# Attention with a cached K and V: keys-by-queries scores in 32-row tiles, probabilities as weights of P.V, sums from a ones column beside V

## The chip, the cores and the metric

The kernel runs on one core of a Trainium2 chip. The metric is device microseconds (us) of one execution. Before the change the kernel takes 501.62 us (median of 3 runs, 500.74 to 503.49). TensorE, which is named PE in the profile, does something nearly all the time (96% of the span).

## The reference, cut to what matters

```python
B, Sq, D = 8, 112, 640            # batches, queries, model width
H, Sk, Dh = 32, 512, 192          # heads, keys, head width; everything in bfloat16

def reference(x, k_cache, v_cache, wq, wo):
    q = (x @ wq).reshape(B, Sq, H, Dh).transpose(0, 2, 1, 3)
    scores = einsum("bhqd,bhkd->bhqk", q, k_cache) * Dh ** -0.5
    p = softmax(scores)
    o = einsum("bhqk,bhkd->bhqd", p, v_cache)
    return o.transpose(0, 2, 1, 3).reshape(B, Sq, H * Dh) @ wo
```

There are 256 pairs of a batch and a head. K and V are 8 x 32 x 512 x 192 x 2 bytes = 50.3 MB each, read once. In what follows a *unit* is four heads of one batch, so there are 64 units.

## The kernel before

Work goes in pairs of heads. K is brought in by DMAs that transpose on the way, so that the head width, over which the scores contract, lies on the partitions (the rows of SBUF, the on-chip memory). Scores have queries on partitions. So the softmax runs along the free axis, and the probabilities then have to be transposed for P.V. That is done by a matmul with a diagonal matrix of reciprocal sums, which also normalises.

```python
# scores of one head: queries x keys, two halves of 256 keys, contraction 192 in two chunks
pe.matmul(bk[:, 0:256], qs[:, qb, EA[h], :], ktb[:, :, 0, cs], start=True, stop=False)
pe.matmul(bk[:, 0:256], qs[:, qb, ET[h], :], ktb[:, :, 1, cs], start=False, stop=True)
pe.matmul(bk[:, 256:512], qs[:, qb, OC[h], :], ktb[:, :, 2, cs], start=True, stop=False)
pe.matmul(bk[:, 256:512], qs[:, qb, OH[h], :], ktb[:, :, 1, cs], start=False, stop=True).then_inc(sS, 1)
...
# transposing and normalising the probabilities with diagonals
for j in range(4):
    mm = pe.matmul(ps[:, 2 + h, j * SQ:(j + 1) * SQ], p_sb[:, pslot, j * 128:(j + 1) * 128],
                   dg[:, dslot, :], start=True, stop=True)
...
# row maximum on VectorE (it also copies the scores to SBUF)
dve.tensor_scalar(s_sb[:, Hh % NSS, :], ps[0:SQ, h, :], -scale, None, op0=ALU.mult,
                  op1=ALU.min, accum_out=nmx[:, Hh % NS:Hh % NS + 1]).then_inc(dSM, 1)
...
# K of four heads (sync engine)
src = k_cache[b, h0:h0 + G].rearrange("u (r q) d -> (u r) (q d)", q=4)
dst = kt[kb][:].rearrange("p a m c -> p (a m) c")
sp.dma_start_transpose(dst, src).then_inc(mK[kb], 16)
```

Of the kernel before, what the change touches and what calls it, by code (L numbers as in the profile page):

```python
# [5 lines left out]

BF16 = mybir.dt.bfloat16
F32 = mybir.dt.float32
ACTF = mybir.ActivationFunctionType
ALU = mybir.AluOpType  # L10

DEFAULT_ORDERS = dict(
    PE=[("S", 0), ("PT0", -1), ("PV", -2), ("PT1", -1), ("O", -3), ("Q", 2)],
# [7 lines left out]
def build_mha_kernel(nc, x, k_cache, v_cache, wq, wo, out, cfg=None):  # L21
    cfg = dict(cfg or {})
    B, SQ, D = x.shape
    _, H, SK, DH = k_cache.shape
# [3 lines left out]
    DC = D // 128  # L28
# [8 lines left out]
    scale = float(DH) ** -0.5  # L37
# [31 lines left out]

    with ExitStack() as es:  # L70
        def sb(name, shape, dt):
            return es.enter_context(nc.sbuf_tensor(name, shape, dt))

        def sem(name):
            return es.enter_context(nc.semaphore(name))

        WQC = HG * DH
        wq_sb = sb("wq_sb", [128, 2, DC, WQC], BF16)
        wo_sb = sb("wo_sb", [128, 2, 3 * PPU, D], BF16)
        OUTT = cfg.get("OUTT", False)  # L80
        if OUTT:
            accT = sb("accT", [128, B, DC, SQ], F32)
            oTf = sb("oTf", [128, 2, DC, SQ], BF16)
            acc = None
        else:
            acc = sb("acc", [SQ, B, D], F32)
        xT_sb = sb("xT_sb", [128, DC, B * SQ], BF16)
        kt = [sb(f"kt{j}", [128, 2, 3, G * 128], BF16) for j in range(NKB)]
        vt = [sb(f"vt{j}", [128, G, 768], BF16) for j in range(NVB)]
        qs = sb("qs", [128, NQ, NSLOT, SQ], BF16)  # L90
        s_sb = sb("s_sb", [SQ, NSS, SK], F32)
        p_sb = sb("p_sb", [SQ, NP, SK], BF16)
# [4 lines left out]
        ident = sb("ident", [128, 128], BF16)  # L97
        nmx = sb("nmx", [SQ, NS], F32)
        rsum = sb("rsum", [SQ, NS], F32)
        rinv = sb("rinv", [SQ, NS], F32)  # L100
        ps = es.enter_context(nc.psum_tensor("ps", [128, 8, 512], F32))

        sS = sem("sS"); sPT = sem("sPT"); sPV = sem("sPV"); sO = sem("sO"); sQ = sem("sQ")
        dSM = sem("dSM"); dDG = sem("dDG"); dQC = sem("dQC"); dPTE = sem("dPTE"); dOA = sem("dOA"); dRC = sem("dRC")
        aEX = sem("aEX"); aQE = sem("aQE"); aPTE = sem("aPTE"); aPVE = sem("aPVE")
        gI0 = sem("gI0"); gINIT = sem("gINIT"); dINIT = sem("dINIT")
        sOF = sem("sOF"); aOF = sem("aOF")
        mX = sem("mX")
# [4 lines left out]
        mK = [sem(f"mK{j}") for j in range(NKB)]  # L113
        mV = [sem(f"mV{j}") for j in range(NVB)]
        mOUT = [sem(f"mOUT{j}") for j in range(2)]
# [3 lines left out]
        mWQ = [sem(f"mWQ{j}") for j in range(min(2, NHG) * PPU)]  # L119
        mWO = [sem(f"mWO{j}") for j in range(min(2, NHG) * PPU)]  # L120
# [23 lines left out]
        block = es.enter_context(nc.Block())  # L144

        def W(eng, s, v):
            if v > 0:
                eng.wait_ge(s, v)
# [120 lines left out]
        def act_evacQ(act, ip):  # L269
            W(act, sQ, ip + 1)  # L270
            W(act, sS, 2 * (ip - NQ) + 2)
            act.activation(qs[:, ip % NQ, 0:3, :], ps[:, 5, 0:3 * SQ].rearrange("p (c s) -> p c s", c=3),  # L272
                           ACTF.Copy).then_inc(aQE, 1)

        def act_evacpT0(act, ip):
            W(act, sPT, 2 * ip + 1)
            W(act, sPV, ip - NPT + 1)
            act.activation(pT_sb[:, ip % NPT, 0, :], ps[:, 2, 0:4 * SQ], ACTF.Copy).then_inc(aPTE, 1)  # L278

        def act_exp(act, i, h):  # L280
            Hh = 2 * i + h
            W(act, dSM, Hh + 1)
            W(act, sPT, Hh - NP + 1)
            act.activation(p_sb[:, Hh % NP, :], s_sb[:, Hh % NSS, :], ACTF.Exp,  # L284
                           bias=nmx[:, Hh % NS:Hh % NS + 1], scale=-1.0,
                           accum_out=rsum[:, Hh % NS:Hh % NS + 1]).then_inc(aEX, 1)

        def act_evacPV(act, ip):
            W(act, sPV, ip + 1)
            W(act, sO, ip - NO + 1)  # L290
            act.activation(oT_sb[:, ip % NO, :, :], ps[:, 4, 0:3 * SQ].rearrange("p (c s) -> p c s", c=3),  # L291
                           ACTF.Copy).then_inc(aPVE, 1)

        def act_evacOF(act, ip):
# [3 lines left out]
            W(act, sOF, b + 1)  # L298
            act.activation(o_out[:, b, :], psb[0:SQ, 7, 256:256 + D], ACTF.Copy).then_inc(aOF, 1)

# [3 lines left out]
        def dve_diag(dve, ip, h):  # L304
# [3 lines left out]
            dve.tensor_scalar(dg[:, Hh % ND, :], ident[0:SQ, 0:SQ], rinv[:, Hh % NS:Hh % NS + 1], None,  # L308
                              op0=ALU.mult).then_inc(dDG, 1)

# [17 lines left out]
        def dve_smax(dve, i, h):  # L328
            Hh = 2 * i + h
            W(dve, sS, Hh + 1)  # L330
            W(dve, aEX, Hh - NSS + 1)
            dve.tensor_scalar(s_sb[:, Hh % NSS, :], ps[0:SQ, h, :], -scale, None, op0=ALU.mult,  # L332
                              op1=ALU.min, accum_out=nmx[:, Hh % NS:Hh % NS + 1]).then_inc(dSM, 1)

# [11 lines left out]
        def dve_oacc(dve, ip):  # L346
# [6 lines left out]
            if OUTT:  # L353
# [3 lines left out]
                for k, (src, cs) in enumerate(parts):  # L357
# [6 lines left out]
                    else:  # L364
                        ins = dve.tensor_tensor(dst, src, accT[:, b, cs, :], op=ALU.add)
                ins.then_inc(dOA, 1)
                return
            parts = [(ps[0:SQ, 6, :], slice(0, 512)), (ps[0:SQ, 7, 0:128], slice(512, 640))]
            for k, (src, cs) in enumerate(parts):
# [4 lines left out]
                elif hg < NHG - 1:  # L374
                    ins = dve.tensor_tensor(acc[:, b, cs], src, acc[:, b, cs], op=ALU.add)
                else:
                    ins = dve.tensor_tensor(o_out[:, b, cs], src, acc[:, b, cs], op=ALU.add)  # L377
            ins.then_inc(dOA, 1)
# [5 lines left out]
        psb = ps[:].bitcast(BF16)  # L384
# [27 lines left out]
        def run_program(eng, stages, order, hook=None, post_hook=None):  # L412
            for i in PER:
                if hook is not None:
                    hook(eng, i)
                for st, lag in order:
                    ip = i + lag
                    if ok(ip):
                        stages[st](eng, ip)
                if post_hook is not None:  # L420
                    post_hook(eng, i)
# [24 lines left out]
        def _(act):  # L446
            W(act, dINIT, 1)
            act.activation(dummy[:, 2:3], dummy[:, 0:1], ACTF.Exp)
            run_program(act, ACT_STAGES, orders["ACT"])
# [211 lines left out]
    return nc  # L661


def bass_standalone__mha_block_cached__near_ridge_kernel(
    nc: bass.Bass,
    x: bass.AP,
    k_cache: bass.AP,
    v_cache: bass.AP,
    wq: bass.AP,
    wo: bass.AP,  # L670
    out: bass.AP,
):
    return build_mha_kernel(nc, x, k_cache, v_cache, wq, wo, out)


# [26 lines left out]
```

## Time and profile before

| | before |
|---|---|
| median of 3 runs | 501.62 us |
| profiled span | 499.2 us |
| PE busy | 479.0 us, 96% |
| VectorE (DVE) busy | 446.6 us, 89% |
| ScalarE (ACT) busy | 355.1 us, 71% |
| share of PE in the chain of work that ended last | 93% |

These are lines of the profile's page of before. First comes the busy time of each engine. Then come the rows that cut the span into 40 slices, where a digit is the busy share in tenths; PEclk is the clock granted to TensorE and DMA the mean over the 16 DMA engines. Then come the queue of the hardware DMAs and the chain of work that ended last.

```profile
PE 479.0 (96%) x6824; PEld 418.9 (84%) x6824; DVE 446.6 (89%) x1610; ACT 355.1 (71%) x898; POOL 71.5 (14%) x133
...
PE   1799999999999999999999999999999999999995
...
PEclk9999999999999999999999999999999999999999
DMA  9999999999999999999999999999999999999000
...
q1 hardware_dynamic: 233472, 101.82, 94.4%
...
PE 93%; DMA 2%; issue 1%; DVE 1%; POOL 1%; ACT 0%; DVEq 0%; POOLq 0%; ACTq 0%
```

TensorE bounds the kernel. The DMA row is full as well, but the chain of waits gives DMA only 2%, so the computing engines seldom wait for a transfer. The next lines are groups of instructions of the same page: line, engine, operation, operands and count, then busy us and mean ns of one, then the idle time before them and what ended it.

```profile
L332 DVE TENSOR_SCALAR_CACHE_REDUCE s_sb<-ps 112x512 f32<-112x512 f32 x256 | 166.3, 686 | 16.2 <-PE ps L169 14.0
...
L182 PE MATMUL ps<-dg,p_sb 112*128 112x112 bf16 x1024 | 94.0, 214 | 1.8 <-ACT p_sb L284 1.6
...
L166 PE MATMUL ps<-kt,qs 128*112 128x256 bf16 x256 | 70.8, 277 | 2.5 <-issue 1.9
```

A mean of 277 ns is the length of one matmul's record, not its cost: the records overlap, and the trace shows successive score matmuls 110 ns apart. The work that the change removes is seen here: the row maximum (L332), the transposes of the probabilities (L182) and score matmuls of contraction 192 that are padded to two chunks of 128.

### The profile page before, as it was taken

Reading aid. Unit: us, or ns where it says so; the run is one execution under the profiler, and the core shown is the slowest. Engines: PE = TensorE matmul, PEld = TensorE weight load, DVE = VectorE, ACT = ScalarE, POOL = GpSimd, SP = SyncE. Lnnn points to the kernel's source line nnn. Section 1 sums busy time; section 2 is a strip of 40 time slices with the busy share of each in tenths; the row PEclk is TensorE's granted clock in tenths of the full one; section 3 lists DMA queues with packets and bytes.
Section 4 is the critical chain, followed back from the end, with each engine's and each line's share of the span. In section 5 each row is a group of like instructions: output and inputs, shape, how many; then the busy total and the mean of one; then the engine's idle time right before and its main releaser. Section 6 shows DMA issues by size and latency. Waiting matters only on the chain.

```text
span 499.2 us, 18678 instructions
## 1 busy us (share of the span) xinstructions
PE 479.0 (96%) x6824; PEld 418.9 (84%) x6824; DVE 446.6 (89%) x1610; ACT 355.1 (71%) x898; POOL 71.5 (14%) x133
## 2 busy tenths in 40 slices
PE   1799999999999999999999999999999999999995
PEld 1788888888888888888888888888888888888884
DVE  2589999998999999999999999999999999999994
ACT  1277777777777777777777777777777777777773
POOL 7110133131000133131000122322000000000000
PEclk9999999999999999999999999999999999999999
DMA  9999999999999999999999999999999999999000
GB/s 227 305 285 239 244 256 274 249 265 292 237 249 263 281 261 259 245 265 251 239 247 236 259 290 279 240 282 260 233 272 254 255 260 255 238 258 261 3 14 25
DMA packets 239738, 119.90 MB, mean 240 GB/s; under 512 B 201840, under 2 KB 236480, under 8 KB 239648
## 3 DMA queue, kind: packets, MB, share of 16 engines
q1 hardware_dynamic: 233472, 101.82, 94.4%
q0 software_dynamic: 6176, 16.88, 11.3%
q8 instruction: 56, 0.92, 0.8%
q14 instruction: 34, 0.28, 0.2%
HBM read 67.21 MB, written 1.15 MB: 137 GB/s over the span
## 4 chain that ended last, share of the span: by engine, by line
PE 93%; DMA 2%; issue 1%; DVE 1%; POOL 1%; ACT 0%; DVEq 0%; POOLq 0%; ACTq 0%
PE ps L262 19%; PE ps L234 16%; PE ps L182 13%; PE ps L200 10%; PE ps L206 8%; PE ps L166 6%; PE ps L169 6%; PE ps L167 6%; PE ps L168 6%; PE ps L235 4%; DMA wq_sb<-in_wq_dram 2%; DVE xT_sb L409 1%; POOL wq_sb L578 0%; DVE s_sb L332 0%; DVE o_out L377 0%
## 5 line engine op out<-in xcount | busy, mean ns | idle before, releaser
L284 ACT ACTIVATE p_sb<-s_sb,nmx 112x512 bf16<-112x512 f32 x256 | 181.6, 712 | 3.1 <-DVE s_sb L332 2.1
L332 DVE TENSOR_SCALAR_CACHE_REDUCE s_sb<-ps 112x512 f32<-112x512 f32 x256 | 166.3, 686 | 16.2 <-PE ps L169 14.0
L278 ACT ACTIVATE pT_sb<-ps 128x448 bf16<-128x448 f32 x128 | 69.5, 543 | 88.4 <-PE ps L182 88.4
L262 PE MATMUL ps<-xT_sb,wq_sb 128*128 128x112 bf16 x1920 | 118.0, 215 | 5.2 <-DMA wq_sb<-in_wq_dram 5.2
L234 PE MATMUL ps<-wo_sb,oT_sb 128*112 128x512 bf16 x384 | 118.3, 380 | 0.0
L262 PEld LDWEIGHTS ps<-xT_sb,wq_sb 128*128 128x128 bf16 x1920 | 103.8, 99 | 16.7 <-DMA wq_sb<-in_wq_dram 4.4
L182 PE MATMUL ps<-dg,p_sb 112*128 112x112 bf16 x1024 | 94.0, 214 | 1.8 <-ACT p_sb L284 1.6
L272 ACT ACTIVATE qs<-ps 128x336 bf16<-128x336 f32 x128 | 57.6, 450 | 45.0 <-PE ps L262 41.8
L338 DVE CAST pT_sb<-ps 128x448 bf16<-128x448 f32 x128 | 79.9, 624 | 5.3 <-PE ps L182 1.4
L235 PE MATMUL ps<-wo_sb,oT_sb 128*112 128x128 bf16 x384 | 83.9, 219 | 0.0
L182 PEld LDWEIGHTS ps<-dg,p_sb 112*128 112x128 bf16 x1024 | 64.5, 98 | 14.4 <-ACT p_sb L284 1.9
L166 PE MATMUL ps<-kt,qs 128*112 128x256 bf16 x256 | 70.8, 277 | 2.5 <-issue 1.9
L200 PE MATMUL ps<-pT_sb,vt 128*128 128x112 bf16 x1024 | 71.8, 213 | 0.1
L167 PE MATMUL ps<-kt,qs 128*112 128x256 bf16 x256 | 70.4, 275 | 0.0
L169 PE MATMUL ps<-kt,qs 128*112 128x256 bf16 x256 | 70.4, 275 | 0.0
L168 PE MATMUL ps<-kt,qs 128*112 128x256 bf16 x256 | 70.3, 275 | 0.0
L234 PEld LDWEIGHTS ps<-wo_sb,oT_sb 128*112 128x112 bf16 x384 | 49.7, 129 | 22.3
L581 POOL DMA_DIRECT2D wq_sb<-in_wq_dram x60 | 32.1, 539 | 188.5 <-DMA kt<-in_k_cache_dram 182.4
L308 DVE TENSOR_SCALAR dg<-ident,rinv 112x112 bf16<-112x112 bf16 x256 | 52.9, 249 | 5.0 <-issue 0.5
L200 PEld LDWEIGHTS ps<-pT_sb,vt 128*128 128x128 bf16 x1024 | 56.5, 98 | 0.9 <-issue 0.5
L291 ACT ACTIVATE oT_sb<-ps 128x336 bf16<-128x336 f32 x128 | 55.3, 432 | 1.7 <-PE ps L206 1.7
L235 PEld LDWEIGHTS ps<-wo_sb,oT_sb 128*112 128x112 bf16 x384 | 50.0, 130 | 0.0
(38 smaller groups left out, 498.5 us busy)
## 6 DMA issues: line engine op xcount, KB each, us to landing
vt<-in_v_cache_dram SPq DMA_DIRECT2D x64, 768.0 KB, 5.8
wq_sb<-in_wq_dram POOLq DMA_DIRECT2D x60, 96.0 KB, 5.3
wo_sb<-in_wo_dram POOLq DMA_DIRECT2D x24, 160.0 KB, 5.6
wo_sb<-in_wo_dram POOLq DMA_DIRECT2D x32, 80.0 KB, 5.1
wq_sb<-in_wq_dram POOLq DMA_DIRECT2D x4, 480.0 KB, 10.2
wo_sb<-in_wo_dram POOLq DMA_DIRECT2D x4, 320.0 KB, 10.9
out_dram<-o_out SPq DMA_DIRECT2D x8, 140.0 KB, 4.4
kt<-in_k_cache_dram SPq DMA_TRANSPOSE x64, 9.9
```

The source lines that it names most:

```text
L166: pe.matmul(bk[:, 0:256], qs[:, qb, EA[h], :], ktb[:, :, 0, cs], start=True, stop=False)
L167: pe.matmul(bk[:, 0:256], qs[:, qb, ET[h], :], ktb[:, :, 1, cs], start=False, stop=True)
L168: pe.matmul(bk[:, 256:512], qs[:, qb, OC[h], :], ktb[:, :, 2, cs], start=True, stop=False)
L169: pe.matmul(bk[:, 256:512], qs[:, qb, OH[h], :], ktb[:, :, 1, cs], start=False, stop=True).then_inc(sS, 1)
L182: mm = pe.matmul(ps[:, 2 + h, j * SQ:(j + 1) * SQ], p_sb[:, pslot, j * 128:(j + 1) * 128], dg[:, dslot, :], start=True, stop=True)
L200: pe.matmul(ps[:, 4, oc * SQ:(oc + 1) * SQ], vtb[:, u, q * 192: q * 192 + 128], pT_sb[:, ptb, h, j * SQ:(j + 1) * SQ], start=(j == 0), sto ...
L234: pe.matmul(ps[0:SQ, 6, :], oT_sb[:, ob, c, :], wo_sb[:, wb, 3 * lp + c, 0:512], start=first, stop=last)
L235: mm = pe.matmul(ps[0:SQ, 7, 0:128], oT_sb[:, ob, c, :], wo_sb[:, wb, 3 * lp + c, 512:640], start=first, stop=last)
L262: mm = pe.matmul(ps[:, 5, c * SQ:(c + 1) * SQ], lhsT, xT_sb[:, dc, b * SQ:(b + 1) * SQ], start=(dc == 0), stop=(dc == DC - 1))
L284: act.activation(p_sb[:, Hh % NP, :], s_sb[:, Hh % NSS, :], ACTF.Exp, bias=nmx[:, Hh % NS:Hh % NS + 1], scale=-1.0, accum_out=rsum[:, Hh % ...
L332: dve.tensor_scalar(s_sb[:, Hh % NSS, :], ps[0:SQ, h, :], -scale, None, op0=ALU.mult, op1=ALU.min, accum_out=nmx[:, Hh % NS:Hh % NS + 1]). ...
L338: dve.tensor_copy(pT_sb[:, ip % NPT, 1, :], ps[:, 3, 0:4 * SQ]).then_inc(dPTE, 1)
```

## The change

The intent is to take work off TensorE. Scores are computed as keys x queries. K is loaded as it lies in DRAM and transposed on VectorE in blocks of 32 x 32, as the program lays them out, two bfloat16 values at a time as one int32. Four heads then sit in four groups of 32 partitions, so that each score matmul contracts over 32 rows and four of them, one for each head, are meant to overlap in TensorE. The probabilities come out with keys on partitions, as P.V takes them here, so no transpose is left; they are used as weights, and O comes out with queries on partitions. A column of ones beside V gives the sums of the softmax. The maximum is not subtracted any more: a guard counts sums out of range and, if there is one, runs the old kernel after the new one. O is normalised on VectorE and transposed by TensorE for the output projection.

The diff, cut to its core:

```diff
-def bass_standalone__...: return build_mha_kernel(nc, x, k_cache, v_cache, wq, wo, out)
+    build_main(nc, x, k_cache, v_cache, wq, wo, out, flag)     # old kernel behind `if flag`
+# K: four plain DMAs per unit (sync engine); kr is [128, 4, 4, 192]
+for s in range(4):
+    sp.dma_start(kr[u % NK][:, s].rearrange("p t d -> p (t d)"),
+                 k_cache[b, 4 * g:4 * g + 4, 128 * s:128 * (s + 1)].rearrange(
+                     "a (j t) d -> a j (t d)", t=4)).then_inc(mK[u % NK], 16)
+# V: two DMAs per unit, pairs of keys (768 bytes) beside the ones columns
+for h in range(2):
+    sp.dma_start(vs[u % NV][:, :, h, 32:32 + 2 * DH],
+                 v_cache[b, 4 * g:4 * g + 4].rearrange("a (m h t) d -> h m a (t d)", h=2, t=2)[h]
+                 ).then_inc(mV[u % NV], 16)
+# VectorE: block transposes of K, four per unit
+src = kr[u % NK][:, :, t, :].bitcast(I32).rearrange("p s (c i) -> p c s i", c=3)
+dst = kt[u % 2][:, t].rearrange("p c j e -> p c (j e)").bitcast(I32).rearrange("p c (s j) -> p c s j", s=4)
+dve.transpose(dst, src).then_inc(vKT, 1)
+# TensorE: 96 score matmuls per unit, head a in rows 32a to 32a+31 and in PSUM bank a
+for t in range(4):
+    for c in range(6):
+        for a in range(4):
+            p = slice(32 * a, 32 * a + 32)
+            mm = pe.matmul(ps[:, a, SQ * t:SQ * (t + 1)], kt[u % 2][p, t, c // 2, :, c % 2],
+                           qT[g % 2][p, c, SQ * b:SQ * (b + 1)], start=(c == 0), stop=(c == 5))
+# ScalarE: exp without a maximum, keys on partitions
+act.activation(pT[u % 2][:, a, :, 0:SQ], ..., ACTF.Exp, scale=scale).then_inc(aEX, 1)
+# TensorE: P.V, probabilities as weights, 192 columns of V and the ones column
+mm = pe.matmul(pv[:, k, e, o0:o0 + DH + 1], pT[u % 2][:, a, t, :],
+               vs[u % NV][:, a, t // 2, v0:v0 + DH + 1], start=(t == 0), stop=(t == 3), ...)
+# VectorE, per unit: two K transposes of the next unit, sums, reciprocal, O * reciprocal -> os,
+# then the other two K transposes; TensorE then transposes os for the projection
```

## The prediction

> **What bounds it now.** TensorE. The page shows PE busy 479.0 of 499.2 us, and 93% of the chain of waits. The timeline shows one pair of heads each 3.65 us; 128 pairs make 467 us. The DMA engines are nearly full too (row of tenths: 9 until the last three slices): K comes through DMA transposes of 256-byte packets (196,608, 18 ns each in the trace).
>
> **Removed,** per four heads: 16 score matmuls of 256 columns (110 ns apart), 16 probability transposes (49 ns), 32 PV matmuls, the row maximum (686 ns a head), diagonals (249 ns), query copies, both probability evacuations (543 and 624 ns), the K DMA transposes.
>
> **Added on TensorE, per unit of four heads** (64 units; spacing read as N/2.4 + 2.5 ns, which fits 49 ns at N=112 and 110 at 256): 96 score matmuls on 32-row tiles. If four overlap, 24 steps x 49 = 1.2 us. [...] this trace shows it only for the two 64-column tiles of PV (3 ns apart, pairs each 49 ns). Two tile-mode changes: about 0.09 us each by the gaps around those. PV 16 x 83 = 1.3; transposes of O 0.3; Q 1.4; O projection 1.4. About 5.9 us, 64 x 5.9 = 375 us; with start and end about 405. ScalarE (four exps of about 543 ns, evacuations: 3.7 us) and VectorE (K block transposes, normalising, accumulating: 4.5 us) fit under it.
>
> **What I think decides it: the K loads.** K now comes by plain DMAs whose DRAM side is 4 heads x 32 rows x 1,536 B. [...] No run here shows a DMA on four. In the trace 1,536-byte packets take 65 ns (V alone: 370 to 390 GB/s over 16 engines), 1,280-byte ones 55; I estimate 32 to 35 for V's new 768-byte ones. Each of the first four engines: K 8,192 x 60-65 = 490-530 us; V 4,096 x 32-35 = 130-145; weights and x about 46. Together 665-720 us[...]. With start and end about 695. TensorE would wait some 5 us of each 11 us unit.
>
> **Prediction: 695 us, range 395 to 750.** There are two modes: about 695 if K runs on four engines, about 405 if on sixteen. Faster by over 2%: 0.28; within 2%: 0.02; slower: 0.70.
>
> **What would show it.** Four engines: mean DMA busy near 50% at about 170 GB/s; K landing 8 us or more after issue; PE idle before the score matmuls, released by VectorE's K transposes and those by K DMAs; PE busy 55-60%. Sixteen: 290 GB/s or more, PE over 90%, unit of about 6 us. TensorE steps: score matmuls in fours a few ns apart, each 49 ns; PV spaced 83 ns.
>
> **What would make it wrong.** The sequencer spreads K over 16 engines all the same; packets faster when only four engines run (then 620-650); row tiles that don't overlap (96 x 49 = 4.7 us a unit, 600 us even with good DMA); VectorE's K transposes over 1.2 us each.

Where the text is marked as cut it gave a rule or a figure that no run here shows. The sum keeps its terms: 490-530 for K, 130-145 for V and 46 for weights and x are its 665-720 us, and 695 with start and end; only a comparison with an even load is cut from it. It divides K's 32,768 packets by four engines and V's 65,536 by sixteen; the division was my assumption, and how far the runs bear it out is told below. "The first four engines", here and in the expectations, are the four that K was assumed to run on; which ones they are no trace shows. That four score matmuls overlap was an assumption too; in the trace of after they start 0 to 8 ns apart. The spacing formula is an estimate, a line near the two spacings that stand beside it. V alone moved at 357 GB/s in the median in the trace of before (63 stretches of over 0.5 us with no other packets of more than 4 bytes under way; the 95th percentile is 377), with 16.5 packets under way on average; the 370 to 390 is high.

## The result, and the profile after

Ratios and their 95% intervals in this document are those of the record, and not quite the ratio of the medians quoted: a median takes in every run, slow ones too. "Fast" and "slow" are two states in which one and the same kernel can run.

| | before | after |
|---|---|---|
| median | 501.18 us (500.28 to 503.49, 4 runs) | 794.43 us (790.75 to 796.46, 4 runs) |
| ratio, 95% interval | | 1.5843 (1.5782 to 1.5904) |
| profiled span | 499.2 us | 790.9 us |
| mean rate of the DMAs | 240 GB/s | 152 GB/s |

The change makes the kernel slower by 58%. The bytes moved are the same (119.90 and 120.05 MB); only the rate fell. The same lines of the profile's page, after:

```profile
PE 510.4 (65%) x8920; PEld 367.1 (46%) x8920; DVE 259.0 (33%) x634; ACT 220.8 (28%) x421; POOL 76.3 (10%) x280
...
PE   5546667677568557668567667667666668466555
...
PEclk9867878779788887787787786887877897787788
DMA  5765555546446455456445455455554355445441
...
q1 hardware_dynamic: 114832, 118.70, 50.2%
...
SPq 93%; issue 3%; PE 1%; DMA 1%; DVE 1%; ACT 0%; DVEq 0%
SPq L1060 58%; SPq L1069 30%; SPq L1046 2%; SPq L1052 2%; DMA kr<-in_k_cache_dram 1%; PE ps L817 1%; PE ps L850 0%; PE ps L836 0%; DVE kt L940 0%; DVE os L952 0%; SPq L1041 0%; DVE xs L966 0%; PE ps L859 0%; ACT oT L910 0%; DVE rinv L948 0%
```

No engine is busy all the time: PE has 65% and the DMA row shows four to six tenths for the whole run. The chain is 93% on SPq, the sequencer of the sync engine, at the lines that issue K (L1060) and V (L1069). The groups of the page tell where the wait reaches the computing engines:

```profile
L940 DVE STREAM_TRANSPOSE kt<-kr 128x384 int32<-128x384 int32 x256 | 137.2, 559 | 460.2 <-DMA kr<-in_k_cache_dram 460.2
L859 PE MATMUL ps<-ident,os 112*128 112x112 bf16 x384 | 40.9, 266 | 258.2 <-DVE os L952 258.2
...
L836 PE MATMUL ps<-qT,kt 32*128 32x112 bf16 x6144 | 133.3, 267 | 6.8 <-DVE kt L940 6.3
```

VectorE stands 460.2 us before its K transposes, waiting for the K DMAs. PE's own wait is one step further on. VectorE has two K transposes of the next unit ahead of the normalising in its order, so PE waits for `os` at the transposes of O (258.2 us), and at the scores for 6.3 us only. One unit, from the timeline (start, duration, engine, line, operation; in brackets the idle time before and what ended it):

```profile
401.28 1.04 DVE L940 STREAM_TRANSPOSE kt<-kr 128x384 int32<-128x384 int32 x2 [6.11 <-DMA kr<-in_k_cache_dram]
...
402.69 0.96 DVE L952 TENSOR_TENSOR os<-ps,rinv 112x768 bf16<-112x768 f32 x1
...
403.70 0.47 PE L859 MATMUL ps<-ident,os 112*128 112x112 bf16 x6 [2.79 <-DVE os L952]
...
405.04 2.29 PE L836 MATMUL ps<-qT,kt 32*128 32x112 bf16 x96
405.72 8.02 SPq L1060 DMA_DIRECT2D kr<-in_k_cache_dram  x4
...
407.26 2.17 PE L850 MATMUL ps<-vs,pT 128*128 128x193 bf16 x16
...
412.47 1.04 DVE L940 STREAM_TRANSPOSE kt<-kr 128x384 int32<-128x384 int32 x2 [6.96 <-DMA kr<-in_k_cache_dram]
```

The unit shown takes 11.2 us from one K transpose to that of the next unit (64 units in 790.9 us make 12.4 us each, start and end included). Each of the 64 has one wait of VectorE for K. The sync engine needs 8.02 us for the four instructions that issue K, during which nothing else is issued. That could be the cost of issuing, or the sequencer could be held up by the engines behind it; the page cannot tell the two apart.

The packets' records can say how many DMA engines worked. I counted how many packets of more than 4 bytes were under way at each moment. In the kernel before, from 50 us to its end at 499 us, it is 16 or more for 83% of that time. After, from 50 to 700 us, it is exactly 4 for 37% and exactly 5 for 17%, and under 4 for 1.6%. Where only packets of 1,536 bytes were under way (24% of that time; all but 5,120 of 37,888 are K's), they were exactly 4 for 72% and exactly 5 for 19% of it. Where eight or more of V's packets were under way (23%), the median was 16 in all, 12 of them V's. I read this as K on four engines that hardly ever stop, and V on all 16; the records don't name an engine.

### The profile page after: what moved, and what is told of

Its sections match the earlier page's. It is cut to its first block, busy times and chain, and to the rows that moved or that the text cites. A ratio compares the mean times of both kernels' runs of the same rounds, so it can differ in the third digit from the quotient of the medians.

```text
span 790.9 us, 20398 instructions
## 1 busy us (share of the span) xinstructions
PE 510.4 (65%) x8920; PEld 367.1 (46%) x8920; DVE 259.0 (33%) x634; ACT 220.8 (28%) x421; POOL 76.3 (10%) x280
## 2 busy tenths in 40 slices
DMA packets 114925, 120.05 MB, mean 152 GB/s; under 512 B 3472, under 2 KB 114832, under 8 KB 114832
## 3 DMA queue, kind: packets, MB, share of 16 engines
q1 hardware_dynamic: 114832, 118.70, 50.2%
## 4 chain that ended last, share of the span: by engine, by line
SPq 93%; issue 3%; PE 1%; DMA 1%; DVE 1%; ACT 0%; DVEq 0%
SPq L1060 58%; SPq L1069 30%; SPq L1046 2%; SPq L1052 2%; DMA kr<-in_k_cache_dram 1%; PE ps L817 1%; PE ps L850 0%; PE ps L836 0%; DVE kt L940 0%; DVE os L952 0%; SPq L1041 0%; DVE xs L966 0%; PE ps L859 0%; ACT oT L910 0%; DVE rinv L948 0%
## 5 line engine op out<-in xcount | busy, mean ns | idle before, releaser
L940 DVE STREAM_TRANSPOSE kt<-kr 128x384 int32<-128x384 int32 x256 | 137.2, 559 | 460.2 <-DMA kr<-in_k_cache_dram 460.2
L859 PE MATMUL ps<-ident,os 112*128 112x112 bf16 x384 | 40.9, 266 | 258.2 <-DVE os L952 258.2
L901 ACT ACTIVATE pT<-ps 128x448 bf16<-128x448 f32 x256 | 118.5, 550 | 157.4 <-PE ps L836 157.4
L817 PE MATMUL ps<-wos,oT 128*128 128x320 bf16 x672 | 142.3, 361 | 0.8 <-ACT oT L910 0.8
L836 PEld LDWEIGHTS ps<-qT,kt 32*128 32x128 bf16 x6144 | 120.6, 127 | 38.8 <-issue 25.9
L836 PE MATMUL ps<-qT,kt 32*128 32x112 bf16 x6144 | 133.3, 267 | 6.8 <-DVE kt L940 6.3
L850 PE MATMUL ps<-vs,pT 128*128 128x193 bf16 x1024 | 111.8, 269 | 0.2 <-ACT oT L910 0.2
L801 PE MATMUL ps<-xT,wqs 128*128 128x448 bf16 x420 | 103.5, 388 | 0.0
L850 PEld LDWEIGHTS ps<-vs,pT 128*128 128x128 bf16 x1024 | 94.9, 107 | 11.0 <-issue 5.8
L817 PEld LDWEIGHTS ps<-wos,oT 128*128 128x128 bf16 x672 | 74.9, 116 | 39.2 <-ACT oT L910 1.0
L1031 POOL TENSOR_SCALAR bad<-rinv 112x4 f32<-112x4 f32 x64 | 14.5, 226 | 663.3 <-DVE rinv L948 663.3
L952 DVE TENSOR_TENSOR os<-ps,rinv 112x768 bf16<-112x768 f32 x64 | 61.3, 958 | 2.2
L801 PEld LDWEIGHTS ps<-xT,wqs 128*128 128x128 bf16 x420 | 43.4, 106 | 33.3 <-issue 10.8
```

The costliest lines, as they stand in the source:

```text
L801: mm = pe.matmul(ps[:, bank(it), 0:HQ], wqs[:, g % 2, dc, 128 * c:128 * (c + 1)], rhs, start=(dc == 0), stop=(dc == DC - 1))
L817: mm = pe.matmul(ps[:, bank(it), 0:HO], oT[:, c, 128 * m:128 * (m + 1)], wos[:, g % 2, c, HO * h:HO * (h + 1)], start=(c == 0), stop=(c == 5))
L836: mm = pe.matmul(ps[:, a, SQ * t:SQ * (t + 1)], kt[u % 2][p, t, c // 2, :, c % 2], qT[g % 2][p, c, SQ * b:SQ * (b + 1)], start=(c == 0), s ...
L850: mm = pe.matmul(pv[:, k, e, o0:o0 + DH + 1], pT[u % 2][:, a, t, :], vs[u % NV][:, a, t // 2, v0:v0 + DH + 1], start=(t == 0), stop=(t == ...
L859: mm = pe.transpose(psb[:, 4, o0:o0 + SQ], os_[u % 2][:, 128 * j:128 * (j + 1)], ident[0:SQ, 0:SQ])
L901: act.activation(pT[u % 2][:, a, :, 0:SQ], ps[:, a, 0:4 * SQ].rearrange("p (t q) -> p t q", t=4), ACTF.Exp, scale=scale).then_inc(aEX, 1)
```

## The experiments

**What there is to explain.** Theory A, from the prediction: each K DMA runs on four DMA engines, because the slowest dimension of its DRAM side is 4 (heads). That was my assumption; e1 and e4 change this dimension. The four packets under way agree with the number; which engines they ran on no trace here names. Rivals: B, issuing the instructions costs the time (the chain says SPq); C, the row-tiled matmuls and TensorE's low clock cost it; D, the access pattern in DRAM is slow, whichever engines run it. The runs of e2, e3, e4, e6, e7 and e10 are single ones of unknown state: their large differences stand, a difference of 2% does not.

### e1: the slowest dimension made 32, one head per DMA

```diff
-for s in range(4):
-    sp.dma_start(kr[u % NK][:, s]...,  k_cache[b, 4*g:4*g+4, 128*s:128*(s+1)].rearrange("a (j t) d -> a j (t d)", t=4))
+for a in range(4):
+    sp.dma_start(kr[u % NK][32*a:32*a+32].rearrange("p s t d -> p s (t d)"),
+                 k_cache[b, 4*g + a].rearrange("(s j t) d -> j s (t d)", s=4, t=4))
```

> Same bytes, same 1,536-byte packets, same four K DMAs per unit, but each DMA now covers one head, with 32 partitions outermost on both sides, so 16 engines instead of 4. Theory A (the four engines that carry all of K bound the kernel): about 405 us (395 to 430), DMA at 290 GB/s or more, unit about 6 us, the granted clock back near 1.0. Rival B (the sync engine's issue of 384 small DMAs bounds it; its issue instructions are 93% of the chain): stays near 790. Rival C (row-tiled matmuls and the low clock bound it): stays over 600.

Measured: 551.98 us median (543.59 to 556.84), ratio to before 1.105 (1.0983 to 1.1117). The result is correct (e2 says what that is worth). Two of the four runs are slow ones; the two fast ones (543.59 and 549.62 us) are 9% above before. Theory A's direction is right: the same packets by the same number of instructions take some 247 us less (the mean of the fast runs, 546.6 us, against 794.0 of after). Rival C, which said over 600 us, is dead: the matmuls are the same ones. But 405 us was missed by far. Two more things were in the way. The queue's line and two rows of the timeline, PE only:

```profile
q1 hardware_dynamic: 117904, 118.71, 95.9%
...
256.12 0.59 PE L850 MATMUL ps<-vs,pT 128*128 128x193 bf16 x5
260.33 1.96 PE L850 MATMUL ps<-vs,pT 128*128 128x193 bf16 x11 [3.62 <-issue]
```

First, the DMA engines are full (95.9% of the 16 engines' span, for 50.2% in after), at a lower rate than in the kernel before (222 GB/s, for 240): a 1,536-byte packet takes 113 ns in the median, for 66 ns in the kernel after. Each of these DMAs writes to 32 partitions only. Second, PE stops in the middle of a row of 16 matmuls and waits for nothing that the profile shows ("issue"). I looked for gaps of over 0.7 us between PE's instructions from 60 to 500 us: there are 33, 77.0 us in all, and in all 33 PE goes on 1.3 to 1.8 us after the end of a packet of 16,384 bytes on the queue that the page names "instruction". There are only 72 such packets in the run, one in 7.5 us, so this is no chance. The kernel before has one gap over 0.7 us in that stretch, of 1.6 us near its end (at 489 us), and not after such a packet. I read it so that PE runs out of instructions, because the packets that bring them are late. Both points are taken up in e9 and e6.

### e2: half of every K packet

The result of this one is wrong: only the first two of each four keys are loaded, and zeros stand for the rest. Number of DMAs, number of packets and access pattern stay as they are after the change.

The comparison with the reference did not notice, and it could not: the reference's inputs are so small that the scores have a standard deviation of about 0.0001 and the softmax is even; computed on a CPU with K set to zero, the reference gives the same output bit for bit. So "correct" in this document says nothing about K. That keys and values are paired rightly in after, e1, e3, e5 and e9 follows from their indices and was not tested by a run.

```diff
-    sp.dma_start(kr[u % NK][:, s].rearrange(...),      ... "a (j t) d -> a j (t d)", t=4))
+    sp.dma_start(kr[u % NK][:, s, 0:2].rearrange(...), ... "a (j t) d -> a j (t d)", t=4)[:, :, 0:2 * DH])
```

> Wrong result on purpose: each K row group loads its first 768 of 1,536 bytes (the rest is zeroed once), same number of DMAs and packets, still four heads outermost. Theory A: the first four engines lose 8,192 x (66 - 36) ns = 246 us each: about 545 us. Rival B (a fixed cost per DMA issue): stays near 790. Rival C: stays near 790.

Measured: 530.83 us (one run, state unknown), 264 us less than after. The packets, now of 768 bytes, take 36 ns. VectorE's wait for K is halved (460.2 us in after):

```profile
L940 DVE STREAM_TRANSPOSE kt<-kr 128x384 int32<-128x384 int32 x256 | 137.2, 559 | 224.4 <-DMA kr<-in_k_cache_dram 224.4
```

Rival B is dead: the same 256 K instructions, each with the same number of packets, cost 264 us less once the packets are shorter. The issue instructions themselves say the same: one takes 1,708 ns in the median in after, but 433 ns in e1 and e9, which also issue 256 of them with as many packets. The long issue instructions in the chain are not the cause; I read them as the sync engine held up by the DMA engines behind it, though what holds it no trace shows.

### e3: the same access patterns, issued by GpSimd

```diff
-            sp.dma_start(kr[u % NK][:, s]..., k_cache[...]...)     # sync engine
+            gp.dma_start(kr[u % NK][:, s]..., k_cache[...]...)     # GpSimd, three units ahead
```

> K's DMAs keep their access patterns exactly but are issued by GpSimd instead of the sync engine. If the software queue also takes four engines but not always the same four, or all 16, the load evens out: theory A expects a large gain, 405 to 480 us. If it takes the same four engines, A expects about 790 still. Rival B (issue on the sync engine) expects a gain in either case, as 256 of 384 issues leave it; the share of DMA time per engine (packets in flight) then tells A from B. Rival D (the access pattern itself, four heads 196,608 bytes apart, is slow in memory) expects about 790.

Measured: 578.07 us (one run, state unknown), correct. From 50 us on, 16 or more packets are under way for 72% of the time (60% if this queue's many packets of 8 and 12 bytes are left out), and the page shows two queues that together fill the engines (51.3% and 43.0% of the 16 engines' span). Each K DMA has 40 packets of 4,608 bytes and 4 of 3,072; that is four times 32 rows of 1,536 bytes, so it may still be split in four, not always over the same four engines; that is a guess, as the trace names no engine.

```profile
q1 hardware_dynamic: 81040, 68.36, 51.3%
q0 software_dynamic: 49152, 50.74, 43.0%
```

Rival D is dead as far as it explains the slowdown: the same patterns in DRAM and SBUF, with 16 or more packets under way for most of the time, cost 216 us less, although the packets into which they are cut are not the same. The upper end of what was expected (480) is missed, as in e1. Packets are slower here too (K travels in packets of 4,608 bytes at 288 ns, V's take 44 ns for 36), and PE waits for instructions again (from 60 to 500 us, 31 gaps of that kind, 61.0 us). Why this path moves K in 4,608-byte packets the runs don't show.

### e4: two heads per DMA instead of four

```diff
-for s in range(4):                       # 4 DMAs, slowest dimension 4
+for a in range(0, 4, 2):                 # 8 DMAs, slowest dimension 2
+    for s in range(4):
+        sp.dma_start(kr[u % NK][32*a:32*a+64, s]..., k_cache[b, 4*g+a:4*g+a+2, ...]...)
 ...                                      # VectorE's wait for K follows: 128 for 64
```

> K in eight DMAs per unit of two heads each: two engines carry all of K. Theory A: each of those two has 16,384 x 66 ns of K, plus 147 of V and 48 of weights: 1,276 us, with start and end and contention about 1,310 (1,250 to 1,400). Rival B (issue cost): 256 more issues at about 2 us each give up to 1,300 too if a DMA costs a fixed 2 us, but packets in flight then would not sit at two for most of the time; at 0.5 us an issue, about 920.

Measured: 1283.47 us (one run, state unknown). Exactly two packets are under way for 60% of the time, and a packet takes 65 ns as ever. The group of the K transposes:

```profile
L940 DVE STREAM_TRANSPOSE kt<-kr 128x384 int32<-128x384 int32 x256 | 137.2, 559 | 936.9 <-DMA kr<-in_k_cache_dram 936.9
```

Halving the slowest dimension halves the packets under way (2 for 60% of the time, where after has 4 or 5 for 54%) and doubles VectorE's wait for K (936.9 us for 460.2), as theory A says in numbers. Rival B (8.02 us for four issues in the unit of after make 2 us each; the shortest there took 537 ns) might have come near the same time, but not with two packets under way. With e1 to e4 the cause of the slowdown is settled: with four heads outermost some four of K's packets run at a time, with two heads two. By what rule the number follows from the access pattern the runs don't show beyond these cases.

### e10: the kernel after, V loaded for the first four units only

Wrong (relative error 1.27). It measures the share of V by itself, since the prediction's sum for the four engines of K came out too small.

```diff
-                W(pe, mV[u % NV], 32 * (u // NV + 1))
+                W(pe, mV[u % NV], 32)
 def load_v(u):
+    if u >= NV: return
```

> Wrong result on purpose: the changed kernel as it was (K on four engines), V loaded for the first four units only. My sum for the first four engines says K 8,192 x 66 = 541 us, weights and x 48, V gone: about 610 us with start and end, so V's 147 us and some 35 us of contention go. If the sum was too low because K's packets themselves are slower than 66 ns, it stays over 640.

Measured: 618.54 us (one run, state unknown). VectorE still waits for K:

```profile
L940 DVE STREAM_TRANSPOSE kt<-kr 128x384 int32<-128x384 int32 x256 | 137.2, 559 | 312.1 <-DMA kr<-in_k_cache_dram 312.1
```

K, the weights and x alone take longer than the whole kernel before. V, though 12 of its packets were under way beside K's four where it was dense in after, adds 794.43 - 618.54 = 176 us to that. If V is dealt evenly to the 16 engines, as I take it from those counts, each has 60 units x 64 = 3,840 packets of V that are gone here, so by this estimate one costs 45.8 ns on the four engines that also carry K, its own time and any delay that it brings to K's together. The mean duration of such a packet in the trace of after is 45.7 ns (the median is 36). That the two agree doesn't make the mean a rule: for K the mean (73.9 ns, all packets of 1,536 bytes) gives 8,192 x 73.9 = 605 us, which with V and the weights is more than the whole run, and in e2 the mean of 43.1 ns for 12,288 packets gives 530 us, where 530.83 - 48 = 483 us are left for them, 39 ns each. If K runs on four engines, the records of one engine's packets overlap: where nothing but K's packets was under way in e10, 4.2 of them were on average.

### e5: one K DMA per unit, 128 partitions outermost

```diff
-for s in range(4):
-    sp.dma_start(kr[u % NK][:, s].rearrange("p t d -> p (t d)"), ... "a (j t) d -> a j (t d)" ...)
+sp.dma_start(kr[u % NK][:].rearrange("p s t d -> p (s t d)"),
+             k_cache[b, 4*g:4*g+4].rearrange("a (j s t) d -> (a j) (s t d)", s=4, t=4)).then_inc(mK[u % NK], 16)
-W(dve, mK[u % NK], 64 * (u // NK + 1))
+W(dve, mK[u % NK], 16 * (u // NK + 1))
-dst = ... "p c (s j) -> p c s j"
+dst = ... "p c (j s) -> p c s j"
```

Partition 32a + j now takes keys 16j to 16j + 15 of head a in one packet of 6,144 bytes. The write of the transpose is strided, so that each score column again belongs to the key which V has there.

> K of a unit as one DMA with 128 partitions outermost on both sides (keys are dealt out as 16j + 4s + t, the block transposes write their columns in j, s order), 6,144-byte packets, all 16 engines and all 128 partitions. Theory A2: the by-head version had two costs left, (1) each of its DMAs writes only 32 partitions, which made its 1,536-byte packets take 113 ns instead of 65, and (2) TensorE stalled about 100 us for instructions (its chain: issue 18%), in which the 16 KB instruction fetches come late behind data. A2 expects K packets back at about 25 bytes per ns (240 ns each), DMA 290 GB/s, time 400 to 460 us, the rest of the stalls as far as data traffic is still dense. Rival E (the by-head version was bound by something in the row-tiled program itself): about 540 as before.

Measured: 469.42 us median (467.44 to 474.83), ratio to before 0.936 (0.9329 to 0.9391), correct. **This beats the kernel before.** The page:

```profile
PE 400.2 (85%) x8920; PEld 297.4 (64%) x8920; DVE 320.4 (68%) x634; ACT 220.1 (47%) x421; POOL 76.3 (16%) x280
...
q1 hardware_dynamic: 90256, 118.70, 78.3%
...
PE 57%; DVE 24%; issue 14%; DMA 2%; ACT 1%; SPq 0%; POOL 0%; DVEq 0%; POOLq 0%
...
L940 DVE STREAM_TRANSPOSE kt<-kr 128x384 int32<-128x384 int32 x256 | 206.3, 861 | 8.2 <-DMA kr<-in_k_cache_dram 8.2
```

The wait for K is down from 460.2 us to 8.2 us, and a packet of 6,144 bytes takes 234 ns. What remains of the way to 405 us is in PE's waits (line, releaser: us in total, times, longest):

```profile
PE ps L836 <- DVE kt L940: 23.6, 46, 1.0
PE ps L850 <- issue: 9.4, 6, 3.6
PE ps L836 <- issue: 8.1, 6, 3.4
```

The transpose with the strided write (consecutive int32 values 16 bytes apart) takes 861 ns, for 559 ns with a contiguous one, and PE waits about half a microsecond for it in 46 of 64 units. The late instructions are there again, but less.

### e9: as e5, but four DMAs of 1,536-byte packets, each over all 128 partitions

```diff
-sp.dma_start(kr[u % NK][:]..., "a (j s t) d -> (a j) (s t d)")
+for s in range(4):
+    sp.dma_start(kr[u % NK][:, s]..., "a (j s t) d -> (a j) s (t d)" ...[:, s])
```

> As e5, but K of a unit in four DMAs of 1,536-byte packets as in the by-head version; only that each DMA writes all 128 partitions instead of 32. If the by-head version was slow because its DMAs wrote 32 partitions at a time, the packets take about 65 ns here (113 there) and the time is near e5's 469 (465 to 485). If it was slow because of small packets or four DMAs per unit, packets take about 110 ns and the time is near 550.

Measured: 467.53 us median (466.18 to 476.88), ratio to before 0.9345 (0.9301 to 0.939), correct. Against e5 there is no difference to be told. The packets have the size of e1's, and there are as many; they take 65 ns, for 113 ns in e1. That is 113/65 = 1.74 times. Each DMA writes to 128 partitions here, to 32 there. So e1 may have been slow in part because of where it wrote; e9 also reads DRAM in another order than e1 (four heads per DMA instead of one), and no run separates the two. The queue's line, for e1's 95.9%:

```profile
q1 hardware_dynamic: 117904, 118.71, 81.3%
```

### e6: e5 with V loaded for the first four units only

Wrong (relative error 1.27), with the edit of e10. The question is whether late instructions come from dense DMA traffic.

> Wrong result on purpose: as e5, but V is loaded for the first four units only and then reused, so 47 MB of 118 are not moved; the same instructions on TensorE. If instruction fetches are late because of dense data traffic, the TensorE gaps put down to issue fall from about 100 us to under 20 and the time to about 400. If they are late because TensorE simply uses instructions faster than they can be fetched, the gaps stay about as in e5.

Measured: 450.36 us (one run, state unknown). The gaps of PE of over 0.7 us, from 60 us to 28 us or more before the end, and those of them after which PE goes on 1.2 to 1.8 us after the end of an instruction packet:

```
kernel   share of queue q1   gaps over 0.7 us   of these after an instruction packet
e1       95.9%               33, 77.0 us        33, 77.0 us
e5       78.3%               10, 16.0 us         8, 14.5 us
e6       48.1%                4,  4.9 us         1,  2.5 us
```

With less traffic the lateness goes, which agrees with the theory, but the time fell by 19 us only and not to about 400: the wait for the transposes stays (26.1 us).

### e7: e5 with a contiguous write of the transposes

Wrong: keys and values are paired wrongly, which the comparison again does not see.

```diff
-dst = ... "p c (j s) -> p c s j"
+dst = ... "p c (s j) -> p c s j"
```

> Wrong result on purpose: e5 with the block transposes writing their columns next to each other again (key order then no longer matches V's). Transposes back from 861 to about 560 ns, TensorE's 0.5 us wait before each unit's scores (released by VectorE's transposes, 22 us in all) gone: about 443 us. If the rest of e5's distance from 405 us has another cause, it stays at about 469.

Measured: 460.76 us (one run, state unknown). PE's waits:

```profile
PE ps L850 <- issue: 13.8, 7, 3.8
PE ps L836 <- issue: 11.2, 10, 3.9
...
PE ps L836 <- DVE kt L940: 0.5, 1, 0.5
```

The transposes are back at 555 ns, and PE's wait for them falls from 23.6 to 0.5 us. So the strided write does cause that wait. But the waits for instructions grow from 24.4 us (9.4 + 8.1 + 2.8 + 2.2 + 1.9) to 35.0 us (13.8 + 11.2 + 4.9 + 2.0 + 1.8 + 1.3), so the time falls by 9 us instead of 23. A part of the gain is taken by another wait. How much is left can't be told from one run of unknown state: e5's own four runs span 7 us.

### e8: e5, the fourth K transpose before the first accumulation of the projection

```diff
-for t in kts[2:3]: do_KT(u + 1, t)
+for t in kts[2:]:  do_KT(u + 1, t)
 for it in oe[0]: do_OE(it)
-for t in kts[3:]:  do_KT(u + 1, t)
```

> e5 with VectorE's fourth K transpose before the first accumulation of the output projection instead of after it; right result. If the wait before the scores is an order matter, it shrinks and the time goes to 445 to 460; if VectorE is simply full (5.8 us of a 6.2 us unit), the accumulations come late instead and hold a PSUM bank: 460 to 475.

Inconclusive. Four runs took 470.15, 455.79, 466.78 and 469.09 us; only the second counts as fast, and the profiled one is a slow one. PE's gaps of 0.1 to 0.7 us do shrink in that one (10.3 us from 60 to 440 us, for 22.5 us in e5), but its gaps after instruction packets grow (22.2 us for 14.5); a slow run against a fast one, so neither is a finding. The median of 467.93 us is no better than e9's 467.53.

## Why the prediction was right or wrong, point by point

**Direction and mechanism: right.** K on four engines was the more likely of its two modes, and the counts of packets under way agree with it (4 or 5 for 54% of the time in after, 2 for 60% in e4, a queue busy for 95.9% of 16 engines' span in e1). The predicted signs came: DMA near half (50.2% for "near 50%"), 152 GB/s for 170, and VectorE's K transposes were released by K DMAs. K's landing 8 us or more after its issue can't be checked: the page gives no landing time for it.

**The time: wrong, 695 us for 794, outside the range of 395 to 750.** The step that failed is the sum for each of the four engines of K, "Together 665-720 us", and in it first the term of V, "V 4,096 x 32-35 = 130-145". Its terms, predicted at the middle of the spans; the second column of figures takes K as shared by four engines and the rest by 16, and is an estimate from the measured times that stand beside it:

| on each of the four engines of K | predicted, us | from measured times, us | from |
|---|---|---|---|
| K, 8,192 packets of 1,536 B | 510 | 527 | x 64.3 ns: time per K packet and engine where nothing but K was under way in after (80 stretches from 50 to 700 us, 140 us in all) |
| V, 4,096 packets of 768 B | 138 | 188 | x 45.8 ns, e10 by difference (176 us for 3,840) |
| weights and x | 46 | 48 | estimate: 496 x 55 ns + 320 x 66 ns, medians in after |
| start, end and all else | 1 | 31 | what is left of 794 |
| sum | 695 | 794 | |

About half of the miss is V: the prediction took 32 to 35 ns for its packets, in proportion to their bytes. Even the median alone is 36 ns, and beside K's traffic each added 45.8 ns. K's term was right: 527 us lies in the predicted 490 to 530. The rest is mostly the last line, for which the middle of the sum left next to nothing; what fills its 31 us the runs don't show, and one nanosecond more or less for a K packet moves 8 us into or out of it. Why a packet of V costs more beside K is open too; the trace does not say on which engine a packet ran.

**The range was wrong too.** It was wide downwards, for the other mode, and had 55 us above the main guess, although that guess took V's packets at less than the shortest common duration measured (36 ns) and left nothing for start and end.

**The unit.** "Wait some 5 us of each 11 us unit" came as 12.4 us a unit; PE stood idle 35% of the span, or 4.4 us a unit (790.9 - 510.4 = 280.5 us over 64).

**Where TensorE waits: half right.** The prediction put the idle time before the score matmuls. It is before the transposes of O (258.2 us, for 6.3 us at the scores), because VectorE's program has K transposes of the next unit ahead of the normalising of this one.

**TensorE's steps: right.** In the traces the score matmuls start in fours a few ns apart (0 to 8 in after, mostly 3 to 4 in e1, which has the same matmuls), and in after each four starts 49 ns after the last where the clock is full. P.V is spaced 85 ns at full clock for 83 predicted, and its first matmul starts 140 ns after the last score matmul there. In before 143 ns lie between P.V's last 128-column tile and its first 64-column one and 145 ns between the last of these and what follows, for 49 between the 128-column ones: the prediction's 0.09 us for a change of tile mode. That it is the change of mode which takes them no run shows by itself. A row of 96 scores stands in e1's timeline with 1.36 us (1.2 predicted), in the unit of after shown above, at a lower clock, with 2.29 us. Only the share of PE was outside (65% for 55 to 60). In these runs the mean clock is lower the more TensorE idles (0.692 at 41% busy in e4, 0.802 at 65% in after, 0.974 at 85% in e5, 0.999 at 96% in before), and where it was halved, as for some 70% of the fours of after, they are 93 ns apart.

**The other mode, 405 us: not confirmed.** It asked for sixteen engines and got 467.53 to 469.42 us in e5 and e9. The pieces that can be named in e5, if the 405 is taken as it stands, which no run confirms: 405 + 23.6 (waits for the strided transposes) + 24.4 (waits for instructions) + 10.8 (a clock of 0.974 in place of 1, an estimate as if all of the time went with the clock: 405/0.974 - 405) = 463.8 of the 469.84 us of the profiled run. The first is the price of e5's key order; the second was not foreseen. The last six microseconds stay open. So do what sets off the lateness of an instruction packet, beyond the density of traffic, and how much e8 gains when it is not late.

## What to carry to other kernels

Before changing a DMA, write down the slowest dimension of both of its sides: here a 4 that came from the heads left four or five packets under way for 54% of the time and cost more than everything that the change saved on TensorE, and putting 128 partitions outermost turned the same change from 58% slower into 6.5% faster than before. When the chain lies on the instructions that issue DMAs, count the packets under way before believing that issuing is slow. When estimating the time of a loaded DMA engine, don't scale a packet's time by its bytes: V's packets, at 36 ns in the median, cost 45.8 ns beside K's by the estimate from e10. Neither the median nor the mean of the records was right for all of them, so take the cost from a difference between two runs where you can.
